# A fused adaLN, H3 long-convolution and mixer-MLP kernel: last inverse stage by single PSUM buffers, a one-column gelu task, fewer load dependencies, and a new task order

## Chip, cores and metric

The kernel runs on one core of a Trainium2 chip. The metric is the device time in microseconds (us) of one execution; the median of several executions is compared. A core has these engines, each with its own instruction queue worked off in order: TensorE (PE) for matmuls, VectorE (DVE), ScalarE (ACT), GpSimd (POOL), and SyncE (SP), whose queue here issues DMA transfers. PE writes to PSUM, from where ACT or DVE fetch the results (an evacuation).

## The reference, cut to what is computed

S = 2048 positions, D = 640 channels, F = 1728, all in bfloat16, batch 1. The six vectors sa, ca, ga, sb, cb, gb come from one small product with the condition vector c. The second branch gets the modulated x; the input B_x is not used.

```python
def _A_ref(q, k, v, shift_k, ssm_k, ssm_D):
    ...                      # k_shift: causal convolution of k with 4 taps
    kv = k_shift * v
    y = irfft(rfft(kv, 2 * S) * rfft(ssm_k, 2 * S))[:S]
    return q * (y + kv * ssm_D)

def _B_ref(x, w1, w2, w3, w4):
    h = gelu(layernorm(x) @ w1)
    ...                      # four channel groups of h shifted by +1, -1, +2, -2 positions
    x1 = x + hs @ w2
    return x1 + gelu(layernorm(x1) @ w3) @ w4

mod = (silu(c) @ w_mod).reshape(1, 6, 1, 640)        # sa, ca, ga, sb, cb, gb
x = A_q
x = x + ga * _A_ref(layernorm(x) * (1 + ca) + sa, A_k, A_v, ...)
return x + gb * _B_ref(layernorm(x) * (1 + cb) + sb, w1, w2, w3, w4)
```

(The first block is written in short: the reference uses FFT routines of length 4096.)

## The kernel before

**The long convolution.** The Fourier transforms are matmuls with trigonometric matrices, which the kernel makes itself from angles (ACT's Sin). For ssm_k and for kv there is a first stage (L407) and a second stage (L427), each evacuated by ACT (L207) or DVE (L209) through one helper, `evac`. k_shift is a product too (L463). The inverse has two stages. In the first, DVE multiplies the spectra (L617, two multiplications for each of ten blocks), PE transforms (L628, L629), and the result is evacuated into the tile T01. The second (`inverse2`, L649 to L670, matmuls L661) reads T01 in 32x32 pieces and gives y for two or three tiles of 128 positions at a time. Its task writes two PSUM buffers, each evacuated on its own.

**The chain of a tile.** There are 16 tiles of 128 positions. With y and a modulated query q (L594 or L592, L601, L602) a tile goes through these steps:

- `chain_a`: product and residual on DVE (L737, L740 with the row sum), the square sum on ACT (`square_sum`, L729), then `ln_finish`. This makes the negative mean on POOL or DVE (L702, L704 for a group of one tile, L702, L706, L707 for two) and the reciprocal standard deviation on POOL (L712 or L714, L715, and L717).
- `chain_b`: modulation on DVE (L751 or L594 and L755, then L756), a second square sum and `ln_finish`.
- `chain_c`: the normed tile (L724 or L594), and its transposition (`turn`): on PE (L772) with an evacuation by ACT (L778) or DVE (L780) for the first groups, by an SP transposing DMA (L765) for the others.
- `mm_w1`: two products (L818, and L828 for the channels past the 128th of each group), with gelu on ACT (L820, L834).
- `mm_w2`: product of the shifted tiles (L873), residual (L880), square sum, `ln_finish`, normed tile (L724, L594) into RH or RK, and `turn`.
- `mm_w3` (L907, gelu L911), `mm_w4` (L937 and the half block L928), the residuals and the gate on DVE (L960, L966, L967), and output stores (L969). The last tile is handled in two halves (L971 to L988).

The tiles go in groups: [0], [1], [2], [3,4], ..., [13,14], [15] up to w1, and [1], [2,3], ..., [14,15], [0] from w2 on, since tile 0 needs its neighbours. The weights w3 and w4 are loaded into the place of T01 (L1009, L1012), once the second inverse stage has read it; x is loaded in parts (`x_load`, L525), and the modulation weights in twelve parts (L487, products L493, evacuated by L504 or L508).

**What sets the order.** Every piece of work is a task (`add`), with an engine or a choice of engines. Tasks name the regions they read and write, and from these come the dependencies. Nothing is scheduled when the kernel is built: a string, ORDER (L26 to L65), lists every task in the order in which it is emitted. An entry is the task's number, the letter of its engine (P PE, A ACT, D DVE, G POOL, S SP), and, for a task that takes PSUM buffers, which of the four (0 to 3). So `432P:12` is task 432 on PE, with buffers 1 and 2. `run` checks that no task stands ahead of one that it depends on. An engine's queue is its tasks in this order, and an engine waits at its next task until that can run. The four PSUM buffers hold 2 x 512 float32 for each partition.

The dependency `y0` (L992) makes the loads of w1, w2 and the third and fourth part of x wait for the evacuated y of the first tile.

Of the kernel before, what the change touches and what calls it, by code (L numbers as in the profile page):

```python
# [15 lines left out]
S, D, F = 2048, 640, 1728  # L16
# [10 lines left out]
0S 2S 19G 18D 50G 20D 21G 23D 22D 25A 4S 3S 1S 6S 27G 29D 36G 37G 28D 5S 8S 9S 11S 68G 10S 69D 24A 26G 88P:0 72G 73D 31A 30A 32D 38G 66D 89A 84P:1 85A  # L27
67D 90P:2 91A 86P:3 87D 39G 40A 102P:0 103A 100P:1 76P:2 70G 104P:0 41D 49G 101A 77A 42G 43G 105A 106P:3 107A 44A 45G 33S 47S 46S 71D 34S 12S 35S 48S
184S 181S 183S 182S 13S 14S 116P:1 92P:2 98P:0 74D 75D 117D 7S 99A 118P:3 119D 114P:0 15S 112P:1 113D 93A 110P:2 16S 115A 111A 96P:3 97A 94P:0 95D
82P:2 83A 80P:1 81A 78P:3 108P:0 51D 109A 52D 54A 56G 57D 53A 122P:2 79D 155P:1 156A 153P:0 154A 151P:3 152A 123D 157P:2 136D 120P:1 121D 173P:0 158A  # L30
55G 174A 171P:3 172A 177P:2 178D 175P:1 176A 161P:0 162D 141P:3 142A 167P:2 168D 147P:1 148A 58G 59G 163P:0 164D 165P:3 166A 137P:2 138A 145P:1 146A
230D 17S 149P:0 150A 190D 188D 126P:3 127D 139P:2 140A 60A 143P:1 199S 144A 124P:0 125D 179P:2 180A 187D 169P:3 170A 234P:1 235A 244P:2 159P:0 160A
128P:3 231D 242P:1 243A 245A 130P:0 61G 62G 186D 63G 64A 238P:1 239A 129D 131D 232D 248P:2 65G 196S 249A 246P:3 247A 185D 189G 191A 252P:0 202S 253A
134P:1 135D 132P:2 133D 236P:3 240P:1 237A 260P:0 261A 233D 250P:2 251A 241D 423D 200P:3 201A 258P:0 259D 319G 208S 192G 268P:2 269A 318S 197P:3 205S
198A 266P:1 267A 272P:2 273D 270P:3 271A 203P:0 284P:1 285A 292P:2 211S 204D 278P:3 279A 417D 276P:0 277A 342S 293D 426D 209P:1 210D 294P:2 295D 226S
290P:3 222G 291A 280P:1 281D 229G 227S 264P:0 274P:2 275D 343G 223G 265A 256P:3 262P:1 420D 206P:0 207D 257A 225G 254P:2 255D 282P:3 263A 286P:0
288P:1 287D 224G 312P:2 220S 283A 289A 212P:3 321D 320D 218G 213D 313A 328D 304P:0 305A 308P:1 316P:2 317A 217S 216G 302P:0 219S 214G 418D 228S 298P:2
215S 324P:3 325D 309A 221G 327G 326S 329D 322P:1 303A 336D 306P:0 299A 421D 323A 310P:2 296P:3 307A 334S 335G 337D 350S 297A 311A 300P:1 330P:0 301A
351G 332P:3 344D 345D 331A 314P:2 333A 315A 359G 340P:1 341A 338P:0 352D 348P:3 349A 353D 346P:2 358S 347A 360D 361D 354P:1 367G 339A 356P:3 368D 366S
369D 355A 364P:2 357A 375G 362P:0 376D 372P:1 374S 377D 401S 193A 363A 382S 370P:3 373A 384D 383G 385D 380P:0 378P:1 365A 392D 390S 391G 393D 422D  # L40
419D 424D 402P:2 427D 194D 403D 371A 388P:3 381A 379A 407S 389A 428D 386P:0 387A 416G 425D 396P:1 397A 394P:3 395A 398S 399P:0 400D 432P:12 429A 430D
434D 433A 489D 502A 510D 195G 413S 490D 491A 511D 530D 408P:3 513D 404S 405P:0 406A 531D 409A 512A 440S 492G 494D 475P:12 476A 477A 515D 532A 462P:03
463A 410S 411P:1 493G 495D 514G 435S 533D 534G 496A 497D 498G 441G 535D 464A 516D 536D 518D 499D 412A 517A 469P:20 537A 471A 519G 500P:3 538D 539G
414P:1 465G 470A 558D 449S 501D 520D 521P:3 436S 415A 507P:0 522A 443S 559D 560A 540D 541P:2 437S 542A 466P:13 431D 561D 562D 563A 564D 508A 546P:2
467D 468A 547A 548P:1 565G 448S 570D 528P:0 571D 566D 572D 567D 549A 573A 446S 568D 505P:3 506A 569A 574G 575G 447S 509G 529A 503D 523D 504D 621D 622D
472P:21 473A 526P:3 527A 623A 579D 580P:0 581A 576D 439S 543A 524D 577P:2 525D 624D 578D 625D 444S 438S 550P:3 627D 480S 551D 481S 626A 590P:0 591A
445S 482S 552A 588P:2 589A 595P:3 459D 628G 633D 629D 634D 553G 630D 631D 632A 635D 637D 636A 479S 554G 555D 556P:0 557A 592P:2 486S 596D 597A 638G
641A 639D 478S 488G 610P:3 612P:0 611A 593D 608P:2 606P:3 544D 594A 598D 613A 599G 474D 460A 603D 600D 601P:1 604P:0 609A 457D 607A 442S 454A 602A
640S 642S 651P:2 649P:3 461G 650A 450D 487S 652A 485S 605D 673P:0 667P:1 451D 545D 668A 674A 452G 582D 583D 484S 689D 690D 456A 458G 584D 585D 656P:3
692D 693D 653P:2 483S 614P:1 654D 655A 657D 694A 615D 659G 658A 671P:0 695D 660G 664D 665P:2 691A 661D 662P:3 663D 453D 669P:1 696G 701A 702D 703D  # L50
666A 735P:3 455G 672A 670A 697D 698D 699D 705G 737P:2 736A 739P:0 733P:1 616D 704A 643D 644D 645D 700A 738A 706G 709A 675P:32 710S 586D 587D 740A 755D
756D 757A 646A 707D 708S 758D 759D 717P:0 714D 761G 760A 762G 734A 763A 767D 777A 768D 711A 769D 719P:1 764D 780D 676P 718A 720A 721P:0 724P:1 647D
712D 765D 766A 677D 678D 770A 680S 771G 772G 683D 741P:32 648D 773D 774S 722D 775A 776S 785P:0 725D 726A 783P:1 713D 723A 824D 617S 825D 742P 821D
822D 827D 679S 681S 826A 743D 682S 727G 728G 731D 732S 823A 784A 828G 829A 786A 787P:3 729D 730S 833D 834D 835D 830D 831D 832A 837D 684D 685S 836A
620S 838G 790P:1 788D 789A 839D 840S 799P:0 791D 805P:3 806A 781D 841D 715D 716D 881D 749D 793G 792A 882D 842S 883A 803P:1 804A 794G 795A 796S 845P:2
846A 797D 778D 779D 884D 843P:3 844A 885D 887D 800A 801P:1 802A 618S 847P:2 848D 782D 941D 850P:3 851D 852A 886A 849A 619S 687S 798S 865P:0 866A
859P:1 860A 863P:2 807P:30 861P:1 744D 750D 753S 942D 944D 745S 853D 854G 855A 888G 893A 943A 752S 857A 889D 864A 945G 890D 856S 808P 858S 809D 891D
946A 947D 948D 950D 894D 862A 892A 895D 896A 897G 925P:2 926A 898G 751S 815D 747S 919P:3 901D 686S 920A 923P:1 899D 921P:0 949A 951G 922A 902S 900S
905P:2 906A 688S 903P:3 904A 952D 953S 956P:0 957A 954P:2 955A 907P:3 908D 910P:0 810D 958G 748S 959P:2 911D 913G 746S 816D 819S 924A 962P:1 867P:30
960D 817S 963D 813S 754S 912A 993P:2 909A 914G 812S 868P 915D 916S 917D 918S 977P:1 978A 994D 995A 996G 997G 971P:2 820S 972A 869D 998A 875D 927P:30  # L60
818S 964A 814S 811S 876D 961A 965D 966G 973P:1 967A 999S 969A 970S 870D 929D 974A 1028P:2 930D 975P:3 928P 968S 1000P:1 1001A 931S 935D 1002P:0 934S
976A 979P:13 981D 1003A 1006P:0 871S 873S 1004P:1 879S 1005A 872S 874S 936D 980P 987D 1029A 937S 933S 1026P:1 939S 1007A 877S 932S 988D 1024P:2 1025A
1032D 880S 878S 982D 983S 1008P:30 986S 991S 1027A 989S 1033D 1010D 938S 940S 1022P:2 1011D 1023A 1014S 1013S 1009P 1016D 984S 985S 1017D 1030P:13
1034D 992S 990S 1015S 1012S 1018S 1019S 1020S 1035D 1037S 1036S 1021S 1038S 1031P 1040D 1039S 1041D 1043A 1045A 1042S 1044S
# [72 lines left out]
def kernel(  # L137
# [57 lines left out]
    def ca(n):  # L195
        return 0.17 + 0.00083 * n
# [117 lines left out]
    def turns_to(dst, xs, n, r, w, neg=False):  # L314
        sc = (-2.0 if neg else 2.0) * PI_LO
        add("ACT", 0.23 + 0.00083 * n, lambda e: nc.scalar.activation(dst, xs, ACT.Sin, scale=sc), r=[r], w=[w])

    def sin_to(dst, ms, q, n, r, w, neg=False):
        b = (b_neg if neg else b_pos)[dst.start_partition():dst.start_partition() + dst.shape[0], :]
        sc = (2.0 if neg else -2.0) * PI_LO / q  # L320
        add("ACT", 0.25 + 0.00095 * n, lambda e: nc.scalar.activation(dst, ms, ACT.Sin, scale=sc, bias=b),
            r=[r, ("consts", 0, 1)], w=[w])
# [326 lines left out]
    def inverse2(tilesA):  # L649
        n = len(tilesA)  # L650
        pss = [Slot() for _ in range(2)]

        def f(e):
            for s in pss:
                pst(s, name="ps_i2")
            for a, A in enumerate(tilesA):
                for j4 in range(4):
                    for cg in range(4):
                        n1 = 4 * A + cg
                        for cpp in range(2):  # L660
                            nc.tensor.matmul(pss[j4 // 2].tile[32 * cg:32 * cg + 32, j4 % 2, a * 160:(a + 1) * 160],  # L661
                                             lhsT=Hs[32 * j4:32 * j4 + 32, n1, cpp, :],
                                             rhs=Zb[32 * j4:32 * j4 + 32, cpp * 64 + n1, :, :],
                                             start=(cpp == 0), stop=(cpp == 1), tile_position=(32 * j4, 32 * cg))
# [414 lines left out]
```

## Time and profile before

| | us |
|---|---|
| median of 3 runs | 301.24 (301.13 to 302.2) |
| span of the profiled execution | 298.7 |
| PE busy in the span | 269.7 (90%) |
| DVE busy | 218.2 (73%) |
| ACT busy | 208.3 (70%) |
| POOL busy | 104.8 (35%) |

The profiled execution's own time is its span, from the first to the last instruction; what the device time has besides it is 2.54 us. The chain that ended last runs, by engine, 51% over PE, 13% over DVE, 11% over ACT, 10% over DMA and 6% over POOL. The largest waits by group are ACT's L911 for PE's L907 (41.9 us in 14 times; ACT has room there), POOL's L714 for ACT's L729 (28.7 us), and DVE's L960 for PE's L928 (18.1 us).

The table is read by stretches, not by the totals: an engine that is busy for 90% of the whole can be full in one stretch and wait in another. In the profile's lists, a row of a timeline gives the start, the duration of the run of instructions, the engine, the line in the kernel, what is written from what, the count, and in brackets the idle time before it with what ended it. PEclk is the clock granted to PE, 1.00 or 9 being full.

### The profile page before, as it was taken

How to read it: one execution, taken by the hardware profiler on the slowest of the kernel's cores; microseconds unless marked ns; L12 is line 12 of the kernel's file. 1: busy time of each engine (PE TensorE's matmuls, PEld its weight loads, DVE VectorE, ACT ScalarE, POOL GpSimd, SP SyncE). 2: the span in 40 equal slices, each digit the busy share in tenths (PEclk: the TensorE clock that was granted, in tenths of full speed). 3: DMA queues.
4: the chain of work that ended last, by engine and by line, in shares of the span. 5: the costliest groups of instructions: out<-in, count | busy, mean ns of one | idle time of the engine just before them, and what ended most of it. 6: DMA issues, size and time to landing. Idle time of an engine off the chain costs nothing.

```text
span 298.7 us, 7890 instructions
## 1 busy us (share of the span) xinstructions
PE 269.7 (90%) x3176; PEld 208.5 (70%) x3182; DVE 218.2 (73%) x438; ACT 208.3 (70%) x341; POOL 104.8 (35%) x237
## 2 busy tenths in 40 slices
PE   0999999999989766869999999999999999999993
PEld 0666755777878436648878677787788767887871
DVE  8998999999999998898759589886361544212442
ACT  4799989999999789979868775766854705431200
POOL 5864364453216591434275426120421321100000
PEclk9999999999999859799999999999999999999999
DMA  6999999898999920563700203223113030510112
GB/s 215 275 215 184 225 137 246 225 217 221 229 253 281 280 65 2 153 203 69 273 4 0 46 5 68 56 46 60 41 40 80 5 89 6 63 43 23 29 52 60
DMA packets 58356, 35.76 MB, mean 120 GB/s; under 512 B 40032, under 2 KB 55008, under 8 KB 58320
## 3 DMA queue, kind: packets, MB, share of 16 engines
q1 hardware_dynamic: 57136, 32.01, 46.3%
q0 software_dynamic: 1088, 3.21, 4.1%
q8 instruction: 25, 0.41, 0.6%
q14 instruction: 11, 0.09, 0.1%
q10 hardware_dynamic: 96, 0.04, 0.1%
HBM read 16.31 MB, written 2.62 MB: 63 GB/s over the span
## 4 chain that ended last, share of the span: by engine, by line
PE 51%; DVE 13%; ACT 11%; DMA 10%; POOL 6%; issue 5%; SPq 2%; DVEq 0%; POOLq 0%; ACTq 0%
PE ps_w L937 17%; PE ps_w L907 14%; ACT T L207 5%; DMA Ra<-in_A_q_dram 5%; PE ps_w L873 4%; PE ps_w L818 3%; PE ps_s L427 3%; ACT RG L729 3%; DVE Rb L617 3%; PE ps_ksh L463 2%; POOL lnv L715 2%; PE ps_s L407 2%; DMA RK<-R 2%; DVE R L756 2%; PE ps_mod L493 2%
## 5 line engine op out<-in xcount | busy, mean ns | idle before, releaser
L907 PE MATMUL ps_w<-R,T 128*128 128x256 bf16 (+1 forms) x630 | 63.8, 261 | 0.7 <-DMA R<-RH 0.7
L907 PEld LDWEIGHTS <-T 128*128 128x128 bf16 x630 | 55.5, 98 | 7.9 <-issue 2.0
L937 PE MATMUL ps_w<-T,R 128*128 128x320 bf16 x416 | 59.1, 299 | 0.0
L911 ACT ACTIVATE R<-ps_w 128x1024 bf16<-128x1024 f32 (+2 forms) x36 | 28.8, 827 | 41.9 <-PE ps_w L907 41.9
L937 PEld LDWEIGHTS <-R 128*128 128x128 bf16 x416 | 40.5, 98 | 15.2
L960 DVE TENSOR_TENSOR T<-ps_w,R 128x640 bf16<-128x640 f32 x15 | 12.3, 822 | 35.4 <-PE ps_w L928 18.1
L207 ACT CAST T<-ps_s 128x1024 bf16<-128x1024 f32 x32 | 30.4, 1029 | 3.2 <-PE ps_s L407 3.1
L207 ACT CAST R<-ps_s 128x960 bf16<-128x960 f32 (+1 forms) x35 | 30.8, 964 | 1.8 <-PE ps_s L427 1.6
L407 PE MATMUL ps_s<-F1bd,Rb 128*128 128x256 bf16 x160 | 23.3, 298 | 8.7 <-DVE Rb L394 8.1
L729 ACT ACTIVATE RG<-R 128x640 bf16<-128x640 bf16 x32 | 23.5, 734 | 9.9 <-DVE R L880 6.7
L407 PEld LDWEIGHTS <-Rb 128*128 128x128 bf16 x160 | 16.7, 107 | 14.7 <-DVE Rb L394 8.6
L873 PE MATMUL ps_w<-RG,R 128*128 128x320 bf16 x160 | 23.2, 299 | 2.1 <-ACT R L820 2.1
L715 POOL TENSOR_TENSOR lnv<-lnv,mhalf 128x2 f32<-128x2 f32 (+1 forms) x29 | 22.5, 775 | 2.3
L427 PE MATMUL ps_s<-T,RG 64*128 64x160 bf16 x512 | 21.2, 230 | 0.8 <-ACT R L207 0.6
L880 DVE SCALAR_TENSOR_TENSOR R<-ps_w,R 128x640 bf16<-128x640 f32 x16 | 12.9, 819 | 11.8 <-PE ps_w L873 11.6
L427 PEld LDWEIGHTS <-RG 64*128 64x128 bf16 x512 | 17.7, 94 | 5.1 <-issue 4.6
L818 PE MATMUL ps_w<-R,RG 128*128 128x256 bf16 (+1 forms) x200 | 20.0, 259 | 1.3 <-DMA R<-RK 0.6
L873 PEld LDWEIGHTS <-R 128*128 128x128 bf16 x160 | 15.4, 98 | 8.2 <-ACT R L820 2.4
L629 PE MATMUL ps_i<-EB,Rb 128*128 128x128 bf16 x160 | 19.0, 219 | 1.5 <-DVE Rb L617 1.4
L818 PEld LDWEIGHTS <-RG 128*128 128x128 bf16 x200 | 17.1, 102 | 3.5 <-issue 2.0
L628 PE MATMUL ps_i<-EA,Rb 128*128 128x128 bf16 x160 | 19.0, 219 | 0.4 <-ACT R L207 0.3
L714 POOL TENSOR_TENSOR lnv<-stat,lnv 128x2 f32<-128x2 f32 x19 | 4.0, 212 | 40.9 <-ACT RG L729 28.7
(178 smaller groups left out, 513.5 us busy)
## 6 DMA issues: line engine op xcount, KB each, us to landing
Ra<-in_A_ssm_k_dram SPq DMA_DIRECT2D x5, 512.0 KB, 5.7
R<-in_w_mod_dram SPq DMA_DIRECT2D x6, 400.0 KB, 6.0
out_dram<-RH SPq DMA_DIRECT2D x60, 40.0 KB, 1.6
T<-in_B_w_dram SPq DMA_DIRECT2D x5, 432.0 KB, 6.2
RH<-in_w_mod_dram SPq DMA_DIRECT2D x4, 400.0 KB, 4.4
Ra<-in_A_q_dram SPq DMA_DIRECT2D x4, 320.0 KB, 6.6
RK<-R SPq DMA_DIRECT2D x5, 256.0 KB, 4.5
RK<-R POOLq DMA_DIRECT2D x5, 256.0 KB, 5.3
```

The costliest lines, as they stand in the source:

```text
L207: nc.scalar.copy(dst, src(ps.tile))
L407: nc.tensor.matmul(psv[:, ml, :], lhsT=xL[:, s0:s0 + P], rhs=F1r, start=True, stop=True)
L427: nc.tensor.matmul(psv[:, g, j], lhsT=Gs[p, k, 64 - 64 * cc:192 - 64 * cc], rhs=T1h[h][p, cc * 32 + k], start=(cc == 0), stop=(cc == 1), t ...
L628: nc.tensor.matmul(psv[:, w, :], lhsT=Av[:, r_, :, g_], rhs=EAf, start=True, stop=False)
L629: nc.tensor.matmul(psv[:, w, :], lhsT=Bv[:, r_, :, g_], rhs=EBf, start=False, stop=True)
L715: nc.gpsimd.tensor_tensor(rs, rs, mhalf[:, 0:n], ALU.pow)
L729: add("ACT", 0.74, lambda e: nc.scalar.activation(junk, src, ACT.Square, scale=float(D) ** -0.5, accum_out=stat[:, li, 1, t:t + 1]), r=[sk ...
L818: nc.tensor.matmul(pt[:, fb, 0:cw], lhsT=w1_sb[:, b, 160 * fb:160 * fb + P], rhs=hT[:, b, 0:cw], start=(b == 0), stop=(b == ND - 1))
L873: nc.tensor.matmul(pt[:, hf, 0:320], lhsT=gsf[:, fb, c0:c0 + P], rhs=w2_sb[:, fb, 320 * hf:320 * hf + 320], start=(fb == 0), stop=(fb == 4))
L907: nc.tensor.matmul(pt[:, fl, 0:cw], lhsT=w3_sb[:, b, fb * P:(fb + 1) * P], rhs=xT[:, b, 0:cw], start=(b == 0), stop=(b == ND - 1))
L911: nc.scalar.activation(g3[g % 2][:, f0:f0 + fn, 0:cw], ps.tile[:, 0:fn, 0:cw], ACT.Gelu_apprx_tanh)
L937: nc.tensor.matmul(bank(i, hf), lhsT=gg[:, fb, i * P:(i + 1) * P], rhs=w4_sb[:, fb, 320 * hf:320 * hf + 320], start=(fb == 0 and i == 0), ...
```

## The change

It has four parts.

1. ORDER is replaced: all tasks stand in a new order, many with another engine or PSUM buffer. DVE has 291 tasks instead of 301, ACT 246 instead of 248, PE 237 instead of 231, SP 166 instead of 169, POOL 113 instead of 97. The numbers of tasks with the same work differ between the two strings, since tasks were added ahead of them.
2. `inverse2` makes two tasks on PE for each group of tiles, one for each PSUM buffer, with 48 or 32 matmuls each, in place of one task with 96 or 64 that takes two buffers. The matmuls are the same 512.
3. All tasks with a Sin write a new key, "sin". A new ACT task applies gelu to one column (128 x 1) after all of them, and every gelu task depends on it. Where the first gelu stands is where the table of functions is loaded.
4. The dependency `y0` is gone from the loads of w1 and w2 and from two x loads.

Apart from ORDER's lines the diff is this:

```diff
     def turns_to(dst, xs, n, r, w, neg=False):
         sc = (-2.0 if neg else 2.0) * PI_LO
-        add("ACT", 0.23 + 0.00083 * n, lambda e: nc.scalar.activation(dst, xs, ACT.Sin, scale=sc), r=[r], w=[w])
+        add("ACT", 0.23 + 0.00083 * n, lambda e: nc.scalar.activation(dst, xs, ACT.Sin, scale=sc), r=[r], w=[w, ("sin", 0, 1, "s")])
...
     def inverse2(tilesA):
         n = len(tilesA)
-        pss = [Slot() for _ in range(2)]
-
-        def f(e):
-            for s in pss:
-                pst(s, name="ps_i2")
-            for a, A in enumerate(tilesA):
-                for j4 in range(4):
...
-        t1 = add("PE", 0.38 * n, f, r=[("T01", 0, 20480), ("RH", 0, 4096)], alloc=tuple(pss), act=0.2, ni=64 * n)
         yv = y_all[:, tilesA[0]:tilesA[0] + n, :].rearrange("p a (j u) -> p j a u", j=4)
         for i in range(2):
-            t2 = evac(yv[:, 2 * i:2 * i + 2], lambda t: t[:, :, 0:160 * n].rearrange("p j (a u) -> p j a u", a=n), 320 * n, pss[i],
+            ps = Slot()
+
+            def f(e, ps=ps, i=i):
+                pt = pst(ps, name="ps_i2")
+                for a, A in enumerate(tilesA):
+                    for jj in range(2):
+                        j4 = 2 * i + jj
+                        for cg in range(4):
+                            n1 = 4 * A + cg
+                            for cpp in range(2):
+                                nc.tensor.matmul(pt[32 * cg:32 * cg + 32, jj, a * 160:(a + 1) * 160],
+                                                 lhsT=Hs[32 * j4:32 * j4 + 32, n1, cpp, :],
+                                                 rhs=Zb[32 * j4:32 * j4 + 32, cpp * 64 + n1, :, :],
+                                                 start=(cpp == 0), stop=(cpp == 1), tile_position=(32 * j4, 32 * cg))
+            t1 = add("PE", 0.2 * n, f, r=[("T01", 0, 20480), ("RH", 0, 4096)], alloc=ps, act=0.2, ni=32 * n)
+            t2 = evac(yv[:, 2 * i:2 * i + 2], lambda t: t[:, :, 0:160 * n].rearrange("p j (a u) -> p j a u", a=n), 320 * n, ps,
                       [("Rb", D * tilesA[0], D * (tilesA[0] + n), "y")])
             dep(t2, t1)
...
     E0 = 64 + S
+    add("ACT", 0.25, lambda e: nc.scalar.activation(s64[:], b_pos[:], ACT.Gelu_apprx_tanh),
+        r=[("consts", 0, 1), ("sin", 0, 1)], w=[("gelu", 0, 1), ("scol", 0, 1)])
...
         t1 = add("ACT", ca(512 * n), lambda e, ps=ps: nc.scalar.activation(gsf[:, 0:4, c0:c0 + cw], ps.tile[:, :, 0:cw], ACT.Gelu_apprx_tanh),
-                 w=[("gs", t0_, t0_ + n, "gs"), ("R3", 0, 5 * GW, "gs")], use=ps)
+                 r=[("gelu", 0, 1)], w=[("gs", t0_, t0_ + n, "gs"), ("R3", 0, 5 * GW, "gs")], use=ps)
...
     inverse2([0, 1, 2])
-    y0 = [("Rb", 0, D)]
-    dma("SP", 800, lambda q: q.dma_start(w1_sb, B_w1.rearrange("(b p) n -> p b n", p=P)), r=y0, w=[("RG", 0, 3200)])
+    dma("SP", 800, lambda q: q.dma_start(w1_sb, B_w1.rearrange("(b p) n -> p b n", p=P)), w=[("RG", 0, 3200)])
...
-    x_load(8, 12, y0)
-    x_load(12, NT, y0)
+    x_load(8, 12)
+    x_load(12, NT)
```

The other Sin tasks (`sin_to`), the other gelu tasks (`mm_w1`'s second product, `mm_w3`) and the other loads of w2 are changed in the same way. The emitted order follows from ORDER alone. In the changed kernel's emission the 12 tasks of the last inverse stage (two for each of six groups) stand close together on PE. SP's loads of w3 and w4 follow them, with one modulation load (L488 there) among the last of these loads, after two parts of x. The means of the first tiles (L702 and following) stand on POOL.

## The prediction

> **What bounds the kernel now.** I read the page's slices first, then the five slices around the middle with their busy times, then the timelines of PE, DVE, ACT and the DMA queue from 92 to 137 us. The slices show three stretches:
>
> ```profile
> PE   0999999999989766869999999999999999999993
> DVE  8998999999999998898759589886361544212442
> ACT  4799989999999789979868775766854705431200
> PEclk9999999999999859799999999999999999999999
> ```
>
> A slice is 7.47 us. Until 97 us DVE and ACT are full (DVE 93.25 of 97, PE 84.81); from 134 us PE is full and DVE and ACT have room. Between lie five slices in which PE is not full:
>
> ```profile
> core 0: us, PE busy (x) PEld busy (x) DVE busy (x) ACT busy (x) POOL busy (x), PEclk, DMA share, GB/s
> 97.08:104.55 7.47, 5.30 (x237) 3.34 (x217) 7.33 (x18) 5.79 (x12) 4.24 (x7) 0.88 1.08 280
> 104.55:112.02 7.47, 5.17 (x111) 2.86 (x110) 7.11 (x21) 6.44 (x14) 6.96 (x19) 0.50 0.29 66
> 112.02:119.49 7.47, 5.23 (x151) 4.63 (x150) 6.55 (x18) 7.08 (x15) 1.33 (x7) 0.94 0.01 2
> 119.49:126.95 7.46, 6.67 (x151) 5.18 (x149) 6.11 (x15) 7.32 (x19) 3.45 (x12) 0.77 0.53 153
> 126.95:134.42 7.47, 4.65 (x41) 3.47 (x41) 7.19 (x23) 5.98 (x14) 2.79 (x8) 1.00 0.61 204
> ```
>
> DVE's column sums to 34.29 of 37.34: the ramp is set by DVE and the chains that go through it. PE's sums to 27.01, so PE loses 10.3 us here, and some of what it did ran at the granted clock 0.50. After 134.4 PE has 155.85 busy of 157.6: whatever brings the first w3 product forward brings the end forward, unless PE stalls later. So one number carries the forecast, the start of L907, and the way to it is this:
>
> ```profile
> 96.91 1.20 PE L661 MATMUL ps_i<-T,RH 32*32 32x160 bf16 x96 [0.48 <-ACT T L207]
> ...
> 120.50 1.62 PE L661 MATMUL ps_i<-T,RH 32*32 32x160 bf16 x96
> ...
> 125.22 1.52 PE L873 MATMUL ps_w<-RG,R 128*128 128x320 bf16 x10
> ...
> 131.82 1.53 PE L873 MATMUL ps_w<-RG,R 128*128 128x320 bf16 x10 [2.08 <-ACT R L820]
> ...
> 135.74 1.45 PE L907 MATMUL ps_w<-R,T 128*128 128x128 bf16 x23
> ```
>
> The last inverse stage (L661) is strewn over 25 us, from 96.9 to 122.1; the first w3 product comes at 135.74. On DVE the same way is:
>
> ```profile
> 92.57 1.22 DVE L617 TENSOR_TENSOR Rb<-R,RK 128x2048 bf16<-128x2048 bf16 x1
> ...
> 99.56 0.89 DVE L737 TENSOR_TENSOR R<-Rb,RQ 128x640 bf16<-128x640 bf16 x2
> ...
> 116.96 0.45 DVE L594 TENSOR_SCALAR R<-Ra,lnv 128x640 bf16<-128x640 bf16 x1 [0.68 <-POOL lnv L717]
> ...
> 124.07 0.80 DVE L594 TENSOR_SCALAR RK<-R,lnv 128x640 bf16<-128x640 bf16 x2 [1.15 <-POOL lnv L717]
> ...
> 133.60 0.44 DVE L724 TENSOR_SCALAR RH<-R,lnv 128x640 bf16<-128x640 bf16 x1
> ```
>
> From the first L737 (99.56) to the L724 that gives the first w3 product its input (133.60) are 34.0 us, of which DVE idles the 0.68 and 1.15 shown, both behind POOL's L717.
>
> **The change, part by part.** The sum is made against the profiled 298.7 us; the median 301.24 is 2.54 above it, and I carry these 2.54 over unchanged.
>
> *Front, up to the last L617.* The order moves work off DVE. Two angle tasks, a negation of 0.66 and an addition of 0.21 go to POOL, one statistics task (1.04) and one query product (0.46) to others, and one spectrum evacuation of 1.15 to ACT; the second-stage evacuations on DVE go from 8 to 12, the first-stage ones from 8 to 7. By the rows' durations DVE's list up to the last L617 falls from 91.2 to 90.35 us, and ACT's up to the last first-inverse evacuation from 84.3 to 83.9. Against this the first transposed tile (L394) stands behind two more angle tasks, some 1 us later than now, part of it in time in which DVE idles today. I take a gain of 0.5, with bounds +0.85 (all of the DVE time) and -0.6 (the later start in full, 1 us, with half of the gain).
>
> *Last inverse as halves.* An L661 group of 96 is 1.20 us; its first evacuation could not start before the end of it and now can after 48, that is 0.6 us sooner. But today the two evacuations run side by side (ACT 98.01, DVE 98.31, done at 99.45), and the new order gives both of the first tiles to ACT, one after the other. From a PE start at 96.91: first half ready 97.5, then 0.96 and about 0.85 on ACT, 99.4. That is the 99.45 of now: 0, with +0.3 and -0.3 as bounds. PE does 12 halves with the same 512 matmuls in one block; the two-buffer groups waited for a second free buffer, which cost PE, but PE has 10.3 us of idle time here: 0.
>
> *The ramp on DVE.* From the first L737 to the first L724 into RH, the lists of DVE differ as follows: five one-tile mean tasks (two instructions, 0.17 and 0.16) and two of three two-tile ones (L702, L706, L707: 0.50) go to POOL, 2.65 us; the statistics of one pair of tiles (0.88 and 0.21) move out, 1.09; one L602 less, 0.48; one evacuation of 1.14 becomes a smaller one, some 0.3. In come three more transposition copies (L780, 0.48 each, 1.44) and one L594 (0.44). Net 2.6 us less. Filler work now lies between the links of a chain; I let it cover half of the 1.83 us of idle time, 0.9. The mean on POOL lengthens each link: POOL's rows for these are 0.7 and more against 0.33 on DVE. With seven tasks, of which the fillers hide most but not the first of each group (two on the way to L907), that is some 0.8 back. So the ramp gains 2.6 + 0.9 - 0.8 = 2.7, with bounds 4.0 (chains hidden in full: 2.6 + 1.83, less 0.4) and 0.5 (each of seven links pays 0.4, and no idle time goes). If the cover is gone, it is the first w2 products (125.22, 131.82) that come late next.
>
> *Gelu column.* The table load and its consumer are:
>
> ```profile
> 115.56 1.28 ACT L834 ACT_TABLE_LOAD   x1
> 116.85 1.10 ACT L834 ACTIVATE R<-ps_w1x 32x128 bf16<-32x128 f32 x4
> ```
>
> It adds one small ACTIVATE, some 0.25 by the four in 1.10, and moves the 1.28 ahead of the first gelu in ACT's queue. There is one gelu load before and one after; today PE's next L828 waits 1.24 us for this gelu. In the new place the load stands between L729 tasks that feed the chains, so it trades one wait for another. I take -0.2 (bounds +1.2, all of that wait, and -1.5, the load and the column in full in front of an L729). The Trainium skill, "ScalarE: Activation LUTs", section "What ACT_TABLE_LOAD costs", adds a drain of 1.38 us to each load; the rows above show the ACTIVATE starting at the end of the load. By the page the moved cost would be 2.66 and the sum 1.4 worse, 299.2 us.
>
> *Weight loads without the artificial order.* The dropped dependency frees the w1 and w2 loads and the third and fourth x loads from the first evacuated tile. They were not late: w1 was issued at 93.85, landed by 102.3, and its first product is at 114.80. 0. More moves with the block of halves: w3 and w4 overwrite the tile that L661 reads, so they could not be issued before the last L661:
>
> ```profile
> 122.21 0.83 SPq L1012 DMA_DIRECT2D T<-in_B_w_dram  x2
> ```
>
> With all halves in one block (7 us of PE work, paced by 12 evacuations of 0.6 to 0.96 us on two engines) the last ends near 105.5, so they may start some 16 us sooner. Ahead of the last modulation load in SP's queue the new order puts 3.7 MB of these and of x; with its own 0.4 MB 4.2 MB must land. At the 280 GB/s of the first ramp slice that is 15 us (landed 120.5), at the 204 of the last 20.6 (126.1). The product that reads it stands in PE's list about where PE will be at 126.5, so I take 0, with a loss of up to 6.6 (rival C).
>
> *From the first w3 product to the end.* PE's list holds the same 3182 matmuls. Today it loses 1.2 us there, most at 165.7 to 170.8 and 203 to 206.6, behind SP transpositions. Following each buffer's release through the new order, I find the same kind of slack, 0.3 to 5 us, with the tight places at the transposed inputs of w1 for groups 5 and 6 and of w3 for group 3. I take 0.2 more (bounds +0.7, -2.5).
>
> Sum: 0.5 + 0 + 2.7 - 0.2 + 0 + 0 - 0.2 = 2.8, and 0.6 for L907 of the first group now needing only what PE does before it (two of today's L661 groups, 0.6 each of their 1.2 to 1.6, lie between first w1 products and delay them) gives 3.4. Span 298.7 - 3.4 = 295.3, time 297.8 us: -1.1%. The first w3 product would be at about 132.2.
>
> On the clock, the row first: 0.50 between 104.55 and 112.02, where PE had 5.17 us busy with gaps. The Trainium skill, "TensorE: Matmul & The Clock Gate", Part 1, says that an idle window of about 3.4 us drops TensorE to half its clock and that as much sustained work brings it back. That speaks against this change: one block of halves leaves PE with less to do between them and the first w1 products. By the row the 2.6 us of real work done at 0.50 are hidden in PE's idle time and cost 0; by the page the first products, some 10 us of them, could take up to 5 us longer, and the time would be 302.8.
>
> **The rivals.** *B, gained and given back.* L907 comes 3 us sooner, but the late chains don't: POOL takes over means, SP's transpositions start at their old times, and PE, which had 1.2 us of stalls after 135.7, gets 3 more. For: the longest later waits are DMA ones. Against: DVE is busy only 89 of 157.6 us there. Time: 297.8 + 2.9 = 300.7.
>
> *C, the modulation load comes late (slower).* 4.2 MB ahead of an in-order PE. At the 153 GB/s of the slice in which w3 and w4 are loaded today, it lands at 105.5 + 27.5 = 133.0, 6.5 after 126.5, and PE, w2 and w3 products with it, stands still: 297.8 + 6.5 = 304.3. It is slower by the bound from a landing at 131.5 on, that is below 162 GB/s. Against: finer slices of today's loads show 230 to 430 GB/s as soon as two are queued.
>
> *D, it doesn't do what it says.* The halves and the free loads open no time, because DVE's chain is what it was, and only the front's 0.5 is left: 300.5.
>
> **How the numbers follow.** Forecast 0.57, B 0.14, C 0.19, D 0.10. A measurement of this kernel can tell about 0.5% from no change, that is 299.7 to 302.7. The forecast's own range is 294.5 (ramp at 4.0, front at 0.85, halves at +0.3, gelu at +1.2: 3.35 us less) to 300.0 (the ramp alone at 0.5); a twentieth of it lies within the bound. Faster: 0.95 x 0.57 + a third of B and D = 0.62. Same: 0.03 + 0.15 + 0.01 of C = 0.19. Slower: 0.18 of C and 0.01 of B = 0.19. The range from 294.3 to 303.5 leaves out the upper part of C (0.12) and some 0.05 below.
>
> **What would show it.** L907 first near 132 instead of 135.74; last L661 near 105.5; DVE's first L724 into RH near 130; PE's stalls after L907 near 1.4 us; the last modulation product without a wait for a DMA. Wrong would be: a PE wait for the modulation weights or for w3 between 120 and 135, a PE wait of over 1 us for a transposed input after 140, or a first L737 later than 99.6.

## The result, and the profile after

The changed kernel takes 311.37 us (median of 4 runs, 309.85 to 312.72), the kernel before beside it 301.19. The ratio is 1.0329 with a 95% interval of 1.0275 to 1.0384: slower by 3.3%, where 1.1% less was forecast. The profiled execution took 310.18 us with a span of 308.5, 9.8 more than before; 1.7 us lie outside it. In every execution with both on record the device time is 1.65 to 2.2 us longer than the span; the 2.54 us ahead of the prediction set a median against one single execution.

The page's slices of the changed kernel (a slice is now 7.71 us):

```profile
PE   0599999998882974588899989999999999999994
DVE  8999999899982987797779879987222633224033
ACT  3699989899991598879887867876928243220500
PEclk9999999999998695879999999999999999999998
```

The picture has the same three stretches, shifted, and something new at the end of the first: in the thirteenth slice (92.6 to 100.3 us) DVE has a 2 and PE a 2, where the kernel before had nines. The timelines of PE and DVE of the changed kernel give the marks of the prediction:

```profile
145.29 0.89 PE L910 MATMUL ps_w<-R,T 128*128 128x128 bf16 x13
```

```profile
89.40 2.35 DVE L618 TENSOR_TENSOR Rb<-R,R 128x2048 bf16<-128x2048 bf16 x2
98.13 1.22 DVE L618 TENSOR_TENSOR Rb<-R,RG 128x2048 bf16<-128x2048 bf16 x1 [6.38 <-DMA RG<-R]
99.27 1.22 DVE L618 TENSOR_TENSOR Rb<-R,R 128x2048 bf16<-128x2048 bf16 x1
100.40 1.31 DVE L618 TENSOR_TENSOR Rb<-R,RK 128x2048 bf16<-128x2048 bf16 x1
```

The first w3 product (L910 is the old L907) starts at 145.29 instead of 135.74: nearly the whole 9.8 us are lost before it. The second fence shows the largest single piece. DVE stands still for 6.38 us in the middle of its multiplications and waits for a copy into RG. These copies (L614, the old L613) bring each block's spectrum into a second place with its halves exchanged: SP issues one half, POOL the other. POOL's timeline shows why this one is late, first in the changed kernel, then in the kernel before:

```profile
82.35 0.36 POOL L558 TENSOR_TENSOR nb<-mv 128x1 f32<-128x1 f32 x1
82.80 1.05 POOL L559 TENSOR_TENSOR mv<-mv,nb 128x1 f32<-128x1 f32 x1
83.94 1.09 POOL L560 TENSOR_SCALAR rs<-mv 128x2 f32<-128x2 f32 x1
85.12 1.54 POOL L561 TENSOR_TENSOR rs<-rs,mhalf 128x2 f32<-128x2 f32 x1
...
88.38 0.62 POOL L614 DMA_DIRECT2D RK<-R  x1
89.00 0.52 POOL L614 DMA_DIRECT2D RG<-R  x1
```

```profile
82.73 0.51 POOL L613 DMA_DIRECT2D RG<-R  x1 [1.76 <-DVE Rb L617]
85.00 0.51 POOL L613 DMA_DIRECT2D RK<-R  x1 [1.76 <-DVE Rb L617]
```

The copy into RG is needed before the one into RK, and its place is free at 82.7: in the changed kernel SP issues its half at 82.78. POOL's half stands behind the copy into RK in the new order, and both stand behind six layernorm instructions for tiles 4 and 5. It goes out at 89.00, 6.3 us later than before.

The copy itself also took longer. The kernel before, then the changed kernel (DMA views of 78 to 101 us, last number: us from issue to landing):

```profile
RG<-R POOLq DMA_DIRECT2D x1, 256.0 KB, 6.0
```

```profile
RG<-R POOLq DMA_DIRECT2D x1, 256.0 KB, 8.9
```

Before, it landed at 88.7, and its multiplication, at 90.30, waited for nothing:

```profile
90.30 1.22 DVE L617 TENSOR_TENSOR Rb<-R,RG 128x2048 bf16<-128x2048 bf16 x1
```

Of the wait of 6.38 us some 2.9 are thus, as an estimate, the longer copy (8.9 less 6.0), and the rest is the issue's 6.3, less the slack of 1.6 that there was, and less 1.4, since DVE came to this place at 91.7 instead of 90.3.

PE, which follows DVE here, idles as well, and then this happens (windows of 4 us, changed kernel, and PE's timeline):

```profile
core 0: us, PE busy (x) PEld busy (x) DVE busy (x) ACT busy (x) POOL busy (x), PEclk, DMA share, GB/s
96.00:100.00 4.00, 0.59 (x6) 0.60 (x7) 1.87 (x2) 0.00 (x0) 0.52 (x2) 0.82 0.57 160
100.00:104.00 4.00, 4.00 (x41) 4.00 (x39) 3.96 (x9) 2.03 (x2) 2.95 (x5) 0.50 0.85 233
```

```profile
99.41 0.29 PE L630 MATMUL ps_i<-EB,Rb 128*128 128x128 bf16 x1 [6.04 <-DVE Rb L618]
99.48 0.31 PE L629 MATMUL ps_i<-EA,Rb 128*128 128x128 bf16 x1
```

After 6.04 us without work the granted clock is 0.50 ("cold" from here on). The last products of the first inverse stage follow each other at 0.11 us until 105.4, then at 0.055. From the end of the last multiplication to the first L738 (the old L737) it is 8.2 us instead of 5.8.

With the starts of a few lines in the two profiles the 9.8 us can be split (each number is rounded by itself):

| stretch | before | after | difference |
|---|---|---|---|
| to the first multiplication (L617/L618) | 68.4 | 71.8 | +3.4 |
| first to end of last multiplication | 25.4 | 29.9 | +4.5 |
| to the first L737/L738 | 5.8 | 8.2 | +2.4 |
| to the first w3 product (ramp) | 36.2 | 35.4 | -0.8 |
| to the end | 163.0 | 163.2 | +0.2 |

### The profile page after: what moved, and what is told of

Read it like the earlier page. It is cut to its first block, busy times and chain, and to the rows that moved or that the text cites. A ratio compares the mean times of both kernels' runs of the same rounds, so it can differ in the third digit from the quotient of the medians.

```text
span 308.5 us, 7911 instructions
## 1 busy us (share of the span) xinstructions
PE 269.8 (87%) x3182; PEld 212.0 (69%) x3182; DVE 215.4 (70%) x416; ACT 208.7 (68%) x339; POOL 124.8 (40%) x265
## 4 chain that ended last, share of the span: by engine, by line
PE 57%; DMA 10%; DVE 10%; POOL 10%; ACT 7%; issue 3%; SPq 1%; POOLq 0%; DVEq 0%; ACTq 0%
PE ps_w L910 16%; PE ps_w L940 15%; PE ps_w L876 6%; DMA RG<-R 5%; PE ps_ksh L464 4%; PE ps_w L821 4%; PE ps_s L408 3%; POOL lnv L716 3%; PE ps_s L428 3%; ACT T L208 3%; DMA RK<-in_w_mod_dram 2%; DVE Rb L618 2%; ACT RG L730 2%; DMA R<-RK 2%; POOL lnv L705 2%
## 5 line engine op out<-in xcount | busy, mean ns | idle before, releaser
L910 PE MATMUL ps_w<-R,T 128*128 128x256 bf16 (+1 forms) x630 | 63.3, 261 | 0.0
L910 PEld LDWEIGHTS <-T 128*128 128x128 bf16 x630 | 55.7, 98 | 6.5 <-issue 0.5
L940 PEld LDWEIGHTS <-R 128*128 128x128 bf16 x416 | 40.2, 98 | 16.3 <-issue 1.3
L208 ACT CAST T<-ps_s 128x1024 bf16<-128x1024 f32 x33 | 31.6, 1030 | 4.1 <-PE ps_s L408 3.8
L208 ACT CAST R<-ps_s 128x960 bf16<-128x960 f32 (+1 forms) x31 | 27.1, 971 | 1.6 <-PE ps_s L428 1.4
L630 PE MATMUL ps_i<-EB,Rb 128*128 128x128 bf16 x160 | 21.7, 236 | 7.4 <-DVE Rb L618 7.4
L408 PEld LDWEIGHTS <-Rb 128*128 128x128 bf16 x160 | 15.9, 102 | 16.4 <-DVE Rb L395 10.6
L703 POOL TENSOR_SCALAR lnv<-stat 128x2 f32<-128x2 f32 (+1 forms) x21 | 9.0, 429 | 42.2 <-DVE R L883 24.9
L208 ACT CAST T<-ps_i 128x1024 bf16<-128x1024 f32 x20 | 19.3, 1046 | 9.0 <-PE ps_i L630 9.0
L716 POOL TENSOR_TENSOR lnv<-lnv,mhalf 128x2 f32<-128x2 f32 (+1 forms) x29 | 23.1, 797 | 2.3
L821 PE MATMUL ps_w<-R,RG 128*128 128x256 bf16 (+1 forms) x200 | 21.3, 269 | 1.8 <-DVE R L781 1.8
L630 PEld LDWEIGHTS <-Rb 128*128 128x128 bf16 x160 | 17.0, 107 | 8.4 <-DVE Rb L618 8.4
L629 PE MATMUL ps_i<-EA,Rb 128*128 128x128 bf16 x160 | 21.9, 236 | 1.0 <-DVE Rb L618 0.7
L821 PEld LDWEIGHTS <-RG 128*128 128x128 bf16 x200 | 18.4, 107 | 3.5 <-issue 2.1
```

The lines of the kernel that those rows point to most:

```text
L208: nc.scalar.copy(dst, src(ps.tile))
L408: nc.tensor.matmul(psv[:, ml, :], lhsT=xL[:, s0:s0 + P], rhs=F1r, start=True, stop=True)
L629: nc.tensor.matmul(psv[:, w, :], lhsT=Av[:, r_, :, g_], rhs=EAf, start=True, stop=False)
L630: nc.tensor.matmul(psv[:, w, :], lhsT=Bv[:, r_, :, g_], rhs=EBf, start=False, stop=True)
L716: nc.gpsimd.tensor_tensor(rs, rs, mhalf[:, 0:n], ALU.pow)
L821: nc.tensor.matmul(pt[:, fb, 0:cw], lhsT=w1_sb[:, b, 160 * fb:160 * fb + P], rhs=hT[:, b, 0:cw], start=(b == 0), stop=(b == ND - 1))
```

## The experiments

All kernels are made from the two order strings, by moving entries. "New" numbers are those of the changed kernel, whose numbers from 432 on differ from the old ones. Ratios are against the kernel before, run beside them.

| run | median us | ratio (95% interval) | first mult. | end of last | first chain | first w3 |
|---|---|---|---|---|---|---|
| changed kernel | 311.37 | 1.0329 (1.0275 to 1.0384) | 71.8 | 101.7 | 109.9 | 145.3 |
| front_before | 303.21 | 1.0050 (1.0022 to 1.0078) | 69.2 | 94.9 | 103.7 | 140.2 |
| front_after | 312.54 | 1.0345 (1.0290 to 1.0400) | 73.4 | 103.5 | 110.5 | 147.2 |
| pool_later | 308.18 | 1.0201 (1.0143 to 1.0259) | 74.0 | 100.3 | 106.5 | 143.9 |
| w1_later | 311.72 | 1.0312 (1.0262 to 1.0362) | 73.1 | 102.7 | 109.6 | 146.2 |
| copies | 306.58 | 1.0126 (1.0028 to 1.0225) | 75.3 | 99.5 | 106.6 | 141.9 |
| copies_start | 305.66 | 1.0103 (1.0029 to 1.0177) | 74.4 | 99.0 | 105.1 | 140.3 |
| means_dve | 305.82 | 1.0102 (1.0036 to 1.0167) | 73.5 | 98.0 | 103.8 | 140.2 |
| old_order | 302.28 | 1.0010 (0.9978 to 1.0041) | 68.9 | 94.7 | 100.5 | 136.8 |
| x_late | 313.12 | 1.0346 (1.0314 to 1.0379) | 73.1 | 103.6 | 111.6 | 148.1 |
| copies_x | 306.62 | 1.0141 (1.0103 to 1.0180) | 71.9 | 96.8 | 103.1 | 141.8 |
| three_back | 305.98 | 1.0116 (1.0061 to 1.0170) | 73.3 | 96.9 | 103.1 | 140.3 |
| front_before2 | 303.24 | 1.0024 (0.9989 to 1.0058) | 68.5 | 94.0 | 100.9 | 137.9 |
| cut195 | 311.67 | 1.0326 (1.0279 to 1.0373) | 77.8 | 104.4 | 110.6 | 146.3 |
| cut306 | 305.77 | 1.0134 (1.0080 to 1.0187) | 70.1 | 97.7 | 103.6 | 138.8 |
| cut386 | 303.82 | 1.0032 (1.0001 to 1.0062) | 69.7 | 96.9 | 102.8 | 140.2 |
| inj_swap | 306.34 | 1.0134 (1.0088 to 1.0180) | 69.2 | 99.1 | 105.5 | 141.7 |
| inj_ln | 309.03 | 1.0212 (1.0156 to 1.0269) | 68.5 | 99.7 | 107.0 | 144.0 |
| inj_start | 303.15 | 1.0033 (1.0000 to 1.0065) | 70.7 | 95.9 | 101.7 | 137.9 |

The marks are from one profile each. Among the seven kernels with the whole new front the first multiplication lies between 71.8 and 75.3, so differences of 1 to 3 us between two marks say little; the ratios are what counts.

**Front or back, order or code.** The first two exchange the fronts; `old_order` has all of the changed code in the old order.

```diff
 front_before: entries 1 to 417 of the old string, then what is left of the new one
 front_after (in the code of before): the new string up to its first entry of the last inverse stage, then what is left of the old one
 old_order (in the changed code):
-432P:12
+433P:1 435P:2          (and so for each group, old numbers translated)
+432A                   (the gelu column, right ahead of the first gelu)
```

> The changed kernel with the order of the kernel before up to the end of the first inverse stage, and the new order from there on. Theory F (all of the loss is in the front: first multiplication 3.4 us later, one DVE wait of 6.4 us for a copy, and PE cold after it): the first w3 product comes at about 135 us, time 300.5 (299 to 302). Rival T (a good part of the loss sits in the new order behind the front, hidden in the ramp): at least 304.

> The kernel before (pairs of buffers, no gelu column) with the new order up to the end of the first inverse stage, without the early x loads. Theory F: the loss comes along, 311 (309 to 313). Rival T: 304 or less.

> The order of the kernel before in the code of the changed kernel: halves in place of each pair (one behind the other), the gelu column right ahead of the first gelu, the free loads where they stood. Theory O (the order makes all of the loss, the three other parts none): the time of the kernel before within 0.5%. Rival: the halves, each waiting for one buffer, bring the ramp forward by 1 us or more, 300.2 or less; or the parts cost over 0.5%.

The loss goes with the front: 1.0345 with the new front alone, 1.0050 with the new back alone (303.21 us, between its theory's range and its rival's 304). `old_order` equals the kernel before, so halves, gelu column and free loads together make no difference that its interval (0.9978 to 1.0041) would show. In `front_before` the x loads stood ahead of modulation loads at the seam, and the first chain came 8.8 us after the last multiplication. A later run mended that:

> The front of the kernel before and the new order behind it, as in an earlier run, but with the modulation loads ahead of the x loads at the seam, where that run had its last multiplication at 94.9 and its first chain only at 103.7 us. Theory R (the new ramp is worth 0.5 to 1 us over the old): the first chain at 100 to 101, first w3 product near 134.5; 0.3 to 1 us faster than the kernel before. Rival W (the new ramp is worth nothing, since POOL's means cost what DVE gains): within 0.3% of the kernel before, or slower.

With 1.0024 and a ramp of 37.0 us (137.9 - 100.9) where the kernel before has 36.2, the new back is worth nothing over the old: rival W, as far as one can tell.

**The late copy.**

```diff
 pool_later (POOL's entries)
-375G 192G 391G 383G 416G
+375G 391G 383G 192G 416G
 copies
+375G 383G 391G 192G 416G
 w1_later (SP's entries)
-404S 437S 440S 407S
+404S 440S 437S 407S
```

> The changed kernel with one task moved in POOL's queue: the six small layernorm instructions for tiles 4 and 5 (82.35 to 88.44 us) stand behind the last two copies instead of ahead of them. Theory Q (the queue is the cause): the copies are issued near 82.5 and 83.5 instead of 88.4 and 89.0, DVE's wait of 6.4 us shrinks to below 1 and PE stays warm; 304 (302.5 to 305.5). Rival C (the copy is slow because big loads run beside it): half of the wait stays, 308 or more.

> The changed kernel with one load moved in SP's queue: the 800 KB of w1, issued at 88.85 just before POOL's last copy, stand one load further back and so go out at about 99.4. Theory Q: only the copy's 8.9 us shrink, by about a third (2.6 us); 308.7 (307 to 310.5). Rival C: the wait goes almost whole, 305 or less.

> The changed kernel with two entries moved in POOL's queue: the copy into RG (needed two multiplications earlier, its place free from 83 us on) ahead of the copy into RK, and the layernorm instructions for tiles 4 and 5 behind both. Theory Q2 (the copy into RG was queued behind one that could not start, and behind layernorm): DVE's wait of 6.4 us falls below 0.5, PE stays warm; against the changed kernel 6.4 + 2.4 = 8.8 us less at most, so 303.5 (302.5 to 305). Rival C (the transfer itself is slow beside the loads): the wait stays above 2 us, 306 or more.

`pool_later` missed its number: moving only the layernorm left DVE a wait of 2.81 us, since the copy into RK, still ahead, could not go out before 88.50. That showed the second half of the cause, the exchange of the two copies. `w1_later` refutes contention with w1 as the cause: the copy, issued at 90.80, took 8.1 us instead of 8.9 and still kept DVE waiting until 99.09, 5.54 us, and the ratio is that of the changed kernel. Its own theory, a copy shorter by a third and 308.7, missed too. In `copies` the copy goes out at 87.25, the wait is gone, and so is the cold clock. Its DVE timeline and its windows:

```profile
93.69 2.35 DVE L618 TENSOR_TENSOR Rb<-R,R 128x2048 bf16<-128x2048 bf16 x2
95.96 1.22 DVE L618 TENSOR_TENSOR Rb<-R,RG 128x2048 bf16<-128x2048 bf16 x1
97.09 1.22 DVE L618 TENSOR_TENSOR Rb<-R,R 128x2048 bf16<-128x2048 bf16 x1
```

```profile
96.00:100.00 4.00, 3.94 (x64) 3.58 (x62) 4.00 (x6) 3.71 (x5) 3.83 (x3) 1.00 1.10 333
100.00:104.00 4.00, 4.00 (x132) 3.20 (x130) 3.25 (x9) 3.33 (x5) 3.43 (x10) 1.00 1.12 332
```

The time, 306.58, is 1.6 us above the expected range. The order of the queue does not explain why the copy is slow: in `copies_start` and `three_back` (below), where it stands right, it took 8.5 and 8.8 us, but it was issued early enough for that.

**The same cause put into the kernel before.** (Old numbers.)

```diff
 inj_swap
-375G 383G 391G 416G
+375G 391G 383G 416G
 inj_ln (192G taken from its old place)
+375G 192G 391G 383G 416G
 inj_start
-23D 22D 25A ...            (28D 29D further on, 51D 52D behind the first evacuations)
+28D 29D 21G 23D 22D 51D 52D 25A ...
```

> The kernel before with one entry moved: POOL's copy into RK stands ahead of the copy into RG. The copy into RK can't go out before its place is read, near 85 us; the copy into RG, ready at 82.7, then goes out at 85.5 and is needed at 90.3. Theory Q2: 2.8 us late, of which the slack covers some; DVE waits 1 to 2 us, 303.5 (302.5 to 305) against 302.2 before. Rival: the slack covers it all, no change.

> The kernel before with two entries moved: as the run with the swap, and the layernorm instructions for tiles 4 and 5 (6 us on POOL) ahead of both copies. Theory Q2: the copies go out near 88.5 and 89, DVE waits 5 to 6.5 us, PE idles as long and comes back at half its clock (2 us more): 309.5 (307.5 to 311). Rival: 305 or less, the rest of the new order was needed to make the wait.

> The kernel before with the angles in the new order: six pairs ahead of the first transposition, which moves from 6.0 to about 8.5 us. Theory S: DVE is full up to 94 us, so the 2.5 us go through to the end: 304.7 (303.5 to 305.5). Rival: caught up by 30 us, within 0.3% of the kernel before.

DVE's, PE's and POOL's timelines of `inj_ln`:

```profile
96.13 1.23 DVE L617 TENSOR_TENSOR Rb<-R,RG 128x2048 bf16<-128x2048 bf16 x1 [5.62 <-DMA RG<-R]
```

```profile
97.42 0.29 PE L629 MATMUL ps_i<-EB,Rb 128*128 128x128 bf16 x1 [5.34 <-DVE Rb L617]
```

```profile
87.78 0.52 POOL L613 DMA_DIRECT2D RG<-R  x1
```

Two entries of POOL's queue, moved in a kernel that has nothing else of the change, cost 2.1%. The exchange alone (`inj_swap`) costs 1.3%:

```profile
95.53 1.23 DVE L617 TENSOR_TENSOR Rb<-R,RG 128x2048 bf16<-128x2048 bf16 x1 [4.14 <-DMA RG<-R]
```

DVE waits 4.14 us, more than the 1 to 2 expected, since the copy went out at 86.51, not 85.5, and took 8.8 us to land, where the expectation left it the 6.0 of the kernel before. The start costs 0.3%, with an interval that reaches down to nothing; the first transposition moved to 7.1 only, not to 8.5.

**What else was tried of the front.**

```diff
 copies_start: as copies, the first 100 entries from the old string
 x_late: 446S 445S 449S 447S moved behind 410S (447S first there);  copies_x: the same on top of copies
 three_back: copies_start with these x loads late
 means_dve (on top of copies_start)
-520G 540G 504G 525G 545G
+520D 540D 504D 525D 545D
 cut195, cut306, cut386: copies, with so many entries from the old string
```

> As the run with the copies in order, and with the first 100 entries of the order taken from the kernel before (the angles and first transpositions). Theory S (3.4 us of the loss are made in the first 10 us, where the first transposition starts at 8.5 instead of 6.0 us): the first multiplication comes near 69 us instead of 72 to 74; another 3 us less, 300.5 (299 to 302.5). Rival: DVE and ACT catch up or are late again by other waits before 70 us; less than 1 us gained.

> The changed kernel with the four early parts of x (160 KB each, issued at 47.95, 59.20, 70.89 and 86.61 us) moved in SP's queue behind the w1 and w2 loads, where the kernel before has them. Theory X (the early x loads hold up the modulation loads and copies beside them, and with these PE and DVE from 50 to 74 us): the first multiplication comes 1.5 to 3 us sooner; 309 (307.5 to 310). Rival N (they ran in gaps): no change, 311 or more.

> The changed kernel with the copies in order and the x loads late. Theory: both causes add; against the run with the copies in order 1.5 to 3 us less, 304 (303 to 305.5). Rival: as the run with the copies in order, 306 or more.

> Copies in order, x loads late, and the first 100 entries from the kernel before. Theory: what is left of the loss is the start, some 1 to 2 us; 302.5 (301 to 304). Rival: a fourth cause between 20 and 70 us is left, 304.5 or more.

The early x loads are not the cause: without them the ratio stays (1.0346 and 1.0329; 1.0141 and 1.0126). The start taken from the kernel before brings nothing that the intervals part (1.0103 and 1.0126); the 3 us that its theory expected did not come.

> As the run with copies and start, and with five of the six one-tile mean tasks of tiles 0 to 2 on DVE instead of POOL, at the same places of the order. Theory P (POOL is what the ramp waits for now: DVE idles 5.3 us in it instead of 2.95): the work on DVE grows by 1.65 us, its idle time falls by 2 or more; 0.3 to 1.5 us faster than the run with copies and start. Rival D (DVE still sets the ramp): 1 to 2 us slower than it.

Neither theory: 305.82 and 305.66 can't be told apart. What DVE is relieved of by POOL's means is, within the intervals, what it then waits for them.

> The changed kernel with the copies in order, and the first 195 entries of the order from the kernel before (until about 45 us). Theory E (what is left after the copies and the start is lost between 20 and 45 us, in the order of the spectrum evacuations): the first multiplication at 70 us or sooner, 303 (302 to 304.5). Rival L (it is lost later): as copies and start, 305 or more.

> The same with 306 entries (until about 60 us). Theory M (it is lost between 45 and 60 us, where the modulation products stand in PE's queue just when their loads land): 302.5 (301.5 to 304), and the run with 195 entries 305 or more. Rival E: no better than the run with 195 entries.

> The same with 386 entries, until about 90 us: the kernel before nearly up to its last multiplication, and the new order for the last copies' successors and the ramp. Theory R (seam and ramp of the new order are worth as much as the old): 302.3, within 0.4% of the kernel before. Rival W (the new ramp loses 1 us or more by the block of halves and by POOL): 303.5 or more.

As a search for the place of the rest this failed. `cut195` has a stall of its own where the two orders meet (DVE waits 7.37 us at 58.56 for a product), so it tells nothing about the order before that point. `cut386` is faster than `cut306` (1.0032 against 1.0134, the intervals don't meet), but `cut306` too has waits of its own right behind its seam (PE 2.20 us at 76.56). The rest lies most likely in the front, and no place is shown for it. No run beat the kernel before.

## Why the prediction was wrong, step by step

**Front: gain 0.5, bounds +0.85 and -0.6. This is the step that failed; it lost 7.9 us, or 10.3 with the way to the first chain.** The prediction summed DVE's list and ACT's list up to the last L617. It did not follow POOL's queue, though POOL issues half of every copy that DVE's multiplications wait for. 6.4 of the 7.9 us are the wait for one copy, and some 2.9 of these 6.4 are, by the estimate above, the copy's own time, which POOL's queue alone would not have shown. Behind the wait the way to the first chain is 2.4 us longer. The cold PE is 1 to 2 of these: with the same order but for POOL's few entries, and a warm PE, that way is 7.1 us in `copies` and 6.2 in `pool_later`, against 8.2. In `inj_ln` it is 7.3, against 5.8 in the kernel before. `inj_ln` shows the cause by itself: 2.1 of the 3.3 points. One of the prediction's own signs of being wrong came with it, a first L737 after 99.6 (109.86). The list itself was mis-sized by 2 us too: DVE's work up to the end of the last multiplication went from 90.08 to 91.31 us, up by 1.2 instead of down by 0.85, chiefly since the twelve angle instructions (L293, L294; L292, L293 before) of the same sizes took 5.9 us instead of 4.0 (below). DVE also does more of its evacuations before the first multiplication (20 instead of 17), which is why that mark is 3.4 us later with no more idle time on DVE (3.6 us in both).

**What is not settled.** `inj_ln` and `inj_start` make 2.1 + 0.3 of the 3.3 points. The missing 0.9 fits the 1% that `copies` and `copies_start` still lose. Most likely it lies in the order of the front, since the new back alone gives 1.0024 (0.9989 to 1.0058). Whether it is DVE's extra work, modulation products that stood in PE's queue when their loads had not landed (DVE idled 7.1 us before the first multiplication in `copies`), or both, no run parts.

**Halves: 0 at first, and in one block until 105.5.** That they cost nothing (`old_order`) was right. The block was mis-sized: it was to end 6 us after the first chain and ended 11.0 after it, at 120.8, having begun at 107.2. PE stood idle 4.2 us in four gaps between the halves; the profile names no releaser for them. Waiting for PSUM buffers would fit, and is not shown.

**Ramp: 2.7, and 0.6 for L907. It gained 0.8 in this one profile, and nothing in `front_before2`.** The windows of the stretch from the first L738 to the first L725 into RH (after) and from L737 to L724 (before):

```profile
109.86:143.14 33.28, 22.78 (x541) 18.83 (x542) 27.98 (x68) 28.33 (x63) 25.00 (x54) 0.79 0.50 143
```

```profile
99.56:133.60 34.04, 24.21 (x572) 17.41 (x571) 31.09 (x85) 30.53 (x67) 17.35 (x47) 0.80 0.47 130
```

The work term was right: DVE does 3.1 us less (31.09 to 27.98) against 2.6 forecast. The idle term had the wrong sign: -0.9 was forecast for fillers, and idle time grew from 2.95 to 5.30. (The prediction read 1.83 before; those are the two waits that the timeline prints, and the window holds 1.1 more.) The mean on POOL was priced at 0.8 in all; POOL's busy time rose by 7.65 us, and 3.9 us of DVE's idle time now end at POOL's L716 and L718. The stated lower bound of 0.5 does not follow either: seven links at 0.4 are 2.8, which leaves -0.2 of the 2.6. `means_dve` agrees: given back to DVE, five of the means change nothing that shows.

**Gelu column: -0.2.** `old_order`, where the column stands right ahead of the first gelu, shows no cost; its place in the new order was not tried by itself. The ACT timeline of the changed kernel confirms the price of the load and that nothing follows it:

```profile
124.86 1.28 ACT L793 ACT_TABLE_LOAD   x1
126.15 0.20 ACT L793 ACTIVATE s<-b_pos 128x1 f32<-128x1 f32 x1
```

The 1.38 us of drain that the Trainium skill adds ("ScalarE: Activation LUTs", "What ACT_TABLE_LOAD costs") are in neither trace.

**Weight loads: 0.** Right (`w1_later`, `x_late`). Rival C's late modulation load did not come: its product at 140.45 waited for no DMA.

**The end: 0.2 more.** Right: 163.0 to 163.2. Rival B could not be put to the test; nothing was gained ahead of it that could be given back. (Rival D's 300.5 is 300.7 by its own terms, 301.24 less 0.5.)

**The clock.** The prediction looked for cold products behind the block of halves and priced the row at 0. They came elsewhere, behind a stall. An idle time of 2.48 us on PE left the clock at 1.00 (`pool_later`); 3.87 us (`inj_swap`), 4.85 (`front_after`), 5.20 (`w1_later`), 5.34 (`inj_ln`) and 6.04 (changed kernel) all brought 0.50. The Trainium skill, "TensorE: Matmul & The Clock Gate", Part 1, has the mechanism (an idle window of some 3.4 us halves the clock), and these rows agree. Back to full clock it took 2.8 us of continuous products in `inj_swap`, 3.3 in `w1_later`, 3.8 in `front_after`, 4.8 in `inj_ln` (97.4 to 102.2) and 6.0 in the changed kernel (99.4 to 105.4). The 3.4 us that the same part names for this way lie within that range, but do not bound it.

## What to carry to other kernels

A transfer's issue belongs to the queue of the engine that issues it: when an order changes, go through each queue that issues transfers and ask of every entry which of its successors is needed sooner, and whether the entry itself must still wait. Two entries of some 1050 made 2.1 of the 3.3 points here. A stall on an engine that feeds PE can be paid twice, by the wait and by the slow products behind it: here 2.48 us of idle time on PE were not, 3.87 were. And a cause found by taking it out is better shown by putting it alone into the kernel that lacks it.

## What the runs showed of the hardware

Small instructions of DVE and POOL can take many times their usual time beside each other. On DVE this angle instruction of 128x32 took 0.20 us in `inj_start` (at 6.19, beside a POOL instruction of 0.19); beside a POOL instruction of 1.27 us it took 1.29 and ended with it (changed kernel, DVE and POOL):

```profile
6.20 1.29 DVE L294 TENSOR_SCALAR R<-R 128x32 int32<-128x32 int32 x1
```

```profile
6.18 1.27 POOL L311 TENSOR_TENSOR R<-R 128x512 f32<-128x512 f32 x1
```

The other way round, layernorm instructions on one or two columns, which take 0.19 us at the least, took 0.4 to 1.5 beside DVE's multiplications of 1.22 (the POOL timeline above). In `copies`, beside the same multiplications, one took 8.32 and ended within 0.1 us of the last of them, at 99.50:

```profile
91.18 8.32 POOL L558 TENSOR_TENSOR nb<-mv 128x1 f32<-128x1 f32 x1
```

In `pool_later` the same instruction took 4.41 and also ended, at 93.94, within 0.1 us of a row of multiplications. So the time of a small task on POOL lay between 0.2 and 8 us here, and two rows suggest that DVE's work beside it decides; no run takes that work away. The same may be behind the copy's own time from POOL's issue to landing, 8.1 to 8.9 us in the changed kernel, `w1_later`, `inj_ln` and `inj_swap` against 6.0 in the kernel before; that was not tried.
